# Attention steps dealt out behind whole matmul outputs instead of within them

## The chip, the cores and the metric

The kernel runs on one core of a Trainium2 chip. The metric is the device time of one execution in microseconds (us). Five engines of the core matter here: PE (TensorE, matmuls and the loads of their weights), DVE (VectorE), ACT (ScalarE), POOL (GpSimd) and SP (SyncE, which here only issues DMAs). Each engine works through its own list of instructions in order, and semaphores hold one engine until another has got far enough. Matmul results land in PSUM, which the kernel uses as eight banks of 128 x 512 floats.

## The reference

The input x has 2048 tokens of 448 numbers. It is normalised, and two branches of the normalised xn are added to it:

```python
xn = _layernorm(x, axis=-1)
return x + _A_ref(xn, A_wq, A_wk, A_wv, A_wo, A_beta) + _B_ref(xn, B_w_gate, B_w_up, B_w_down)
```

Branch B is a gated feed-forward net, `(sigmoid(xn @ w_gate) * (xn @ w_up)) @ w_down` with 1792 hidden features. Branch A is attention with 16 heads of 28 numbers over four segments of 512 tokens. In each segment a head computes `p = softmax(q k^T * scale + mask)` (the mask leaves a query only the keys at its own place or before it) and `p @ v`, mixes it with what a running memory of the earlier segments recalls (`num / den`, with a gate from beta), and the mixed heads are multiplied by `wo`.

## The kernel before

**Tiling.** Tokens come in four blocks of 512 (`xs[b]`, transposed, 128 features per piece), each of four tiles of 128 tokens. A matrix number is held as a high and a low part, and a product of two such numbers is built from several matmuls that add up in one PSUM bank: eleven for an output with 448 inputs (`TERMS`), six for the sum `down` over two groups of 128 hidden features.

**Stages.** A front part (to about 150 us) normalises x and makes queries, keys and values, and the memory's recall. Then comes the loop, to about 664 us, and then the last output projections. In the loop PE carries two streams that are interleaved by hand:

- the feed-forward net, a generator `gated()`: for each pair of hidden groups `f0`, for each token block `b`, four *outputs* of eleven products (`pgu`, L248: gate and up of each group; each is 128 x 512), and behind each output one *sum* of six products (`pd`, L173, in `down`, 128 x 448), which DVE adds to `acc` (L176). Behind an `up` output ACT takes the tanh of the gate (L256), DVE and ACT make the hidden value `hh` of it (L257, L259, L260).
- attention, a generator `attention()`: 16 *units* (a segment and four heads), each of two *pairs* of heads. A unit has 14 *steps*, listed in `SLOT`. Five steps a pair are scores steps (L612: one 512-wide matmul; or one 384 and one 128 wide; or two 256 wide, into one bank `st`). ACT copies the bank into `w` (L616, L619), POOL masks its diagonal block (L627), DVE takes maxima (L629, L633). When a pair's scores are done, five further *parts* run, one at each of the next five steps: the maxima are combined in a chain of short steps that go between DVE and POOL (L643 to L653), spread out (`mb`, L656), subtracted from `w` in three pieces (L666, DVE), and each piece goes through the exponential (L667, ACT). At step 6 of the next unit comes `finish` with `pa` (L687): 16 products per key block and head, 2.36 us of PE when nothing is late, that read the weights of both pairs.

**Order of the work.** PE and SP follow the order in which the program gives their instructions (`manual_schedule`). The orders of ACT, DVE and POOL are laid out by a scheduler from its own costs. The interleaving is decided by `yield`: the driver at L788 to L794 counts the yields of the feed-forward stream with `k`, and at every yield it runs so many attention steps that the count of steps follows `k` in proportion (234 steps over 541 counts, 0.43 a yield). Before the change an output yields three times (after its 4th, its 8th and its last product) and a sum twice (after its 3rd product and after the addition to `acc`).

**Banks.** Scores rotate through two banks (tag `s`), so a scores step needs the bank of the second scores step ahead of it, which is free once ACT has copied it. `pgu` of the gate and every second `pd` share two banks (`gu`), `pgu` of the up side has two (`p`), the other `pd` one, and `pa` one (`m`).

Of the kernel before, what the change touches and what calls it, by code (L numbers as in the profile page):

```python
# [61 lines left out]
def kernel(  # L62
# [21 lines left out]
    def split(hi, lo, src):  # L84
        A.activation(hi, src, AF.Copy)
        V.tensor_sub(lo, src, hi.bitcast(F32))

    def split_weights(w, raw):
        split(w[:, 0:4, :], w[:, 4:8, :], raw)
# [25 lines left out]
    def bank(name, tag):  # L115
        return ps.tile([P, L], F32, name=name, tag=tag, bufs=banks[tag])
# [29 lines left out]
    def eight_k(dtype, name):  # L146
        return mid.tile([P, 8, 256], dtype, name=name, tag="8k")

    def four_k(dtype, name):
        return mid.tile([P, 2, L], dtype, name=name, tag="4k", bufs=4)  # L150

    def two_k(name):
        return mid.tile([P, L], F32, name=name, tag="2k", bufs=2)
# [7 lines left out]
    def late_pair(name):  # L161
        return late.tile([P, 2, D], F32R, name=name, tag="late")
# [3 lines left out]
    def gated():  # L166

        def down(b, hs, wd, t, tag="pd"):
            tok = slice(t * P, (t + 1) * P)
            mms = [(h[:, a, tok], wd[f][:, w, :]) for f, h in hs for a, w in ((0, 0), (0, 1), (1, 0))]  # L170
            pd = bank("pd", tag)
            for n, (l, r) in enumerate(mms):
                T.matmul(pd[:, :D], l, r, start=n == 0, stop=n == len(mms) - 1)  # L173
                if n == 2:
                    yield
            V.tensor_add(acc[b][:, t, :], pd[:, :D], acc[b][:, t, :])  # L176
            yield

        raw_up, raw_down, wgu, wdn = {}, {}, {}, {}

        def load_up(f):

            raw_up[f] = mid.tile([P, 1024], F32, name="raw", bufs=2)
            if f < NF:
                nc.sync.dma_start(raw_up[f], w_ffn[f][:, :1024])
            else:
                nc.sync.dma_start(raw_up[f][:, :2 * D], w_o[:, 2 * D * (f - NF):2 * D * (f - NF + 1)])

        def load_down(f, tag="rawd"):
            raw_down[f] = (mid.tile([P, 1024], F32, name="raw", bufs=2)[:, :D] if tag == "raw" else  # L190
                           mid.tile([P, D], F32, name="rawd", bufs=1))
            nc.sync.dma_start(raw_down[f], w_ffn[f][:, 1024:])

        def ready_up(f):
            wgu[f] = eight_k(F32R, "wgu")
            split_weights(wgu[f], raw_up[f].rearrange("p (c n) -> p c n", c=4))

        def ready_down(f):
            wdn[f] = late_pair("wdn")
            split(wdn[f][:, 0, :], wdn[f][:, 1, :], raw_down[f])  # L200

        def ready_out(h):
            wo[h] = eight_k(F32R, "wo").rearrange("p c n -> p (c n)")[:, 16:]
            split(wo[h][:, :2 * D], wo[h][:, 2 * D:4 * D], raw_up[NF + h][:, :2 * D])

        begin.extend([lambda: ready_down(0), lambda: (ready_down(1), load_down(2)), lambda: ready_down(2)])
        load_up(0)
        yield
        ready_up(0)
        yield  # L210
        load_up(1)
        load_down(0)
        yield


        todo = [None, None]
        for f0 in range(0, NF, FG):


            ahead = {}  # L220
            if f0 == 0:
                ahead[0, 0] = lambda: (load_down(1, "raw"), ready_up(1))
                ahead[0, 2] = lambda: load_up(2)
                ahead[1, 3] = lambda: load_up(3)
            if f0 + FG < NF:
                ahead[1, 2] = lambda: ready_up(f0 + 2)
                if f0 > 0:
                    ahead[2, 1] = lambda: ready_down(f0 + 2)
                ahead[2, 3] = lambda: load_down(f0 + 3)
                ahead[2, 2] = lambda: load_up(f0 + 4)  # L230
                ahead[3, 2] = lambda: ready_up(f0 + 3)
                ahead[3, 3] = lambda: ready_down(f0 + 3)
                if f0 > 0:
                    ahead[0, 2] = lambda: (load_up(f0 + 3), load_down(f0 + 2))
            else:

                ahead[0, 2] = lambda: load_up(f0 + 3)
                ahead[1, 2] = lambda: ready_out(0)
                ahead[3, 2] = lambda: ready_out(1)
            for b in range(NB):  # L240
                hs = []
                for f in range(f0, f0 + FG):
                    pgu = []
                    for side in range(2):
                        slot = 2 * (f - f0) + side
                        dst = bank("pgu", ("gu", "p")[side])
                        for n, (a, w) in enumerate(TERMS):
                            T.matmul(dst, wgu[f][:, w, side * P:(side + 1) * P], xs[b][:, a, :],  # L248
                                     start=n == 0, stop=n == len(TERMS) - 1)
                            if n in (3, 7):  # L250
                                yield
                        pgu.append(dst)
                        if side == 1:

                            sg = two_k("sg")
                            A.activation(sg, pgu[0], AF.Tanh, scale=0.5)  # L256
                            V.scalar_tensor_tensor(sg, sg, 1.0, pgu[1], op0=ALU.add, op1=ALU.mult)  # L257
                            hh = four_k(F32R, "hh")
                            A.activation(hh[:, 0, :], sg, AF.Copy, scale=0.5)  # L259
                            V.scalar_tensor_tensor(hh[:, 1, :], sg, 0.5, hh[:, 0, :].bitcast(F32),  # L260
                                                   op0=ALU.mult, op1=ALU.subtract)
                            hs.append((f, hh))
                        yield
                        if todo and f0 + b > 0:
                            yield from todo.pop(0) or ()
                        if (b, slot) in ahead:
                            ahead[b, slot]()
                end = f0 + FG == NF and b == NB - 1
                todo += [down(b, hs, wdn, t, ("pd", "s" if end else "gu")[t % 2]) for t in range(NT)]
        rest.extend(todo)  # L270
# [5 lines left out]
    with tc.tile_pool(name="front", bufs=2) as sb, tc.manual_schedule(engines=FRONT):  # L276
# [200 lines left out]
        for t in range(2):  # L477
# [23 lines left out]
                        compare_op=ALU.is_ge, fill=0.0)  # L501

        ffn = gated()
        for b in range(NB):
            last = b == NB - 1
# [23 lines left out]
            for k, c in enumerate((3, 4, 5, 6, 0, 1, 2) if last else range(7)):  # L529
# [34 lines left out]
                n = k - 1 if b == 0 else k + 1  # L564
# [269 lines left out]
```

## Time and profile before

| what | value |
|---|---|
| median of 3 runs | 691.52 us (691.22 to 691.61) |
| the profiled execution's own time | 691.24 us |
| its span, first to last instruction | 689.6 us |
| PE busy over the span | 682.4 us, 99% |
| DVE busy | 569.7 us, 83% |
| ACT busy | 342.6 us, 50% |
| POOL busy | 146.0 us, 21% |

The busy time of PE is that of modelled, overlapping matmuls: what a matmul costs is read from the distance between the starts of neighbours, not from its own duration. In a timeline, consecutive instructions of one kind are merged into a row with a count; the bracket at the end is the idle time of the engine ahead of the row and what ended it. PEld is the loading of matmul weights, which runs ahead of the products.

### The profile page before, as it was taken

Reading aid. Unit: us, or ns where it says so; the run is one execution under the profiler, and the core shown is the slowest. Engines: PE = TensorE matmul, PEld = TensorE weight load, DVE = VectorE, ACT = ScalarE, POOL = GpSimd, SP = SyncE. Lnnn points to the kernel's source line nnn. Section 1 sums busy time; section 2 is a strip of 40 time slices with the busy share of each in tenths; the row PEclk is TensorE's granted clock in tenths of the full one; section 3 lists DMA queues with packets and bytes.
Section 4 is the critical chain, followed back from the end, with each engine's and each line's share of the span. In section 5 each row is a group of like instructions: output and inputs, shape, how many; then the busy total and the mean of one; then the engine's idle time right before and its main releaser. Section 6 shows DMA issues by size and latency. Waiting matters only on the chain.

```text
span 689.6 us, 10445 instructions
## 1 busy us (share of the span) xinstructions
PE 682.4 (99%) x3594; PEld 565.6 (82%) x3594; DVE 569.7 (83%) x994; ACT 342.6 (50%) x563; POOL 146.0 (21%) x349
## 2 busy tenths in 40 slices
PE   8999999999999999999999999999999999999997
PEld 7898888778878787788878878787787878878897
DVE  6765795767889898989898989998889889889863
ACT  5837555343455555544555446455544555446220
POOL 4500020101222122221222223222232322222000
PEclk9999999999999999999999999999999999999999
DMA  7446566696243233333233342324342432333342
GB/s 266 183 146 240 194 224 235 255 331 161 77 102 95 61 86 86 81 112 102 56 71 103 70 123 56 101 55 116 81 114 56 96 72 71 86 95 80 91 155 106
DMA packets 45797, 84.37 MB, mean 122 GB/s; under 512 B 6321, under 2 KB 20401, under 8 KB 45233
## 3 DMA queue, kind: packets, MB, share of 16 engines
q1 hardware_dynamic: 42736, 76.37, 35.9%
q0 software_dynamic: 3008, 7.34, 4.9%
q8 instruction: 28, 0.46, 0.3%
q14 instruction: 25, 0.20, 0.1%
HBM read 51.05 MB, written 32.64 MB: 121 GB/s over the span
## 4 chain that ended last, share of the span: by engine, by line
PE 77%; DVE 10%; issue 7%; POOL 3%; ACT 1%; DMA 1%; SPq 0%; POOLq 0%; ACTq 0%
PE pgu L248 30%; PE pd L173 14%; PE pp L355 10%; PE po L771 5%; PE pv L335 5%; PE st L612 4%; PE pa L687 4%; DVE mx L629 2%; POOL w L627 2%; PE pmm L383 2%; PE n L401 1%; DVE acc L176 1%; DVE w L666 1%; DMA acc<-in_x 1%; PE pt L95 1%
## 5 line engine op out<-in xcount | busy, mean ns | idle before, releaser
L248 PE MATMUL pgu<-xs,wgu 128*128 128x512 f32 x1232 | 316.8, 395 | 0.0
L248 PEld LDWEIGHTS pgu<-xs,wgu 128*128 128x128 f32 x1232 | 226.6, 188 | 45.0 <-issue 3.2
L173 PE MATMUL pd<-wdn,hh 128*128 128x448 f32 x672 | 161.8, 367 | 0.0
L667 ACT ACTIVATE w<-w 128x1024 f32<-128x1024 f32 (+1 forms) x96 | 87.1, 915 | 96.5 <-DVE w L666 95.8
L173 PEld LDWEIGHTS pd<-wdn,hh 128*128 128x128 f32 x672 | 123.0, 188 | 14.5 <-issue 0.6
L627 POOL TENSOR_SCALAR_AFFINE_SELECT w<-w 128x256 f32<-128x256 f32 (+1 forms) x160 | 79.1, 496 | 251.5 <-ACT w L616 216.3
L666 DVE TENSOR_TENSOR w<-w,mb 128x1024 f32<-128x1024 f32 (+1 forms) x96 | 99.7, 1050 | 0.2
L616 ACT ACTIVATE w<-st 128x512 f32<-128x512 f32 x128 | 74.8, 588 | 41.3 <-PE st L612 41.2
L629 DVE TRANSPOSE_TENSOR_REDUCE mx<-w 128x32 f32<-128x1024 f32 x64 | 79.1, 1235 | 12.9 <-POOL w L627 12.8
L355 PE MATMUL pp<-xs,wqk 128*128 128x512 f32 x308 | 77.7, 401 | 0.0
L176 DVE TENSOR_TENSOR acc<-pd,acc 128x448 f32<-128x448 f32 x112 | 67.4, 602 | 2.0 <-PE pd L173 2.0
L355 PEld LDWEIGHTS pp<-xs,wqk 128*128 128x128 f32 x308 | 56.8, 188 | 13.4 <-issue 2.4
L612 PE MATMUL st<-qk 84*128 84x128 f32 (+3 forms) x256 | 64.1, 311 | 0.4 <-ACT w L616 0.3
L259 ACT ACTIVATE hh<-sg 128x512 fp32r<-128x512 f32 x56 | 35.1, 626 | 47.3 <-DVE sg L257 37.3
L612 PEld LDWEIGHTS st<-qk 84*128 84x128 f32 x256 | 48.4, 189 | 9.3 <-ACT w L616 1.9
L256 ACT ACTIVATE sg<-pgu 128x512 f32<-128x512 f32 x56 | 33.2, 593 | 33.4 <-PE pgu L248 32.9
L656 DVE STREAM_TRANSPOSE mb<-top 128x1024 f32<-128x1024 f32 x32 | 39.8, 1243 | 10.3 <-POOL top L653 10.1
L362 DVE TENSOR_TENSOR qk<-pp,qk 128x512 fp32r<-128x512 f32 x28 | 19.3, 688 | 29.8 <-ACT e L360 23.7
L257 DVE SCALAR_TENSOR_TENSOR sg<-sg,pgu 128x512 f32<-128x512 f32 x56 | 37.4, 668 | 4.3 <-PE pgu L248 4.3
L260 DVE SCALAR_TENSOR_TENSOR hh<-sg,hh 128x512 fp32r<-128x512 f32 x56 | 38.4, 685 | 2.4 <-ACT hh L259 2.2
L335 PE MATMUL pv<-wv,xs 128*128 128x448 f32 x176 | 39.8, 376 | 0.2
L687 PE MATMUL pa<-w,vv 128*32 128x128 f32 (+3 forms) x512 | 39.6, 436 | 0.1
(100 smaller groups left out, 637.3 us busy)
## 6 DMA issues: line engine op xcount, KB each, us to landing
qk<-qd SPq DMA_DIRECT2D x192, 112.0 KB
qd<-qk SPq DMA_DIRECT2D x28, 512.0 KB
raw<-in_w_ffn SPq DMA_DIRECT2D x14, 512.0 KB
vd<-vst SPq DMA_DIRECT2D x4, 1024.0 KB
vv<-vd SPq DMA_DIRECT2D x16, 256.0 KB
od<-w POOLq DMA_DIRECT2D x16, 256.0 KB, 3.8
sums<-od SPq DMA_DIRECT2D x32, 128.0 KB
out<-acc SPq DMA_DIRECT2D x16, 224.0 KB
```

The costliest lines, as they stand in the source:

```text
L173: T.matmul(pd[:, :D], l, r, start=n == 0, stop=n == len(mms) - 1)
L176: V.tensor_add(acc[b][:, t, :], pd[:, :D], acc[b][:, t, :])
L248: T.matmul(dst, wgu[f][:, w, side * P:(side + 1) * P], xs[b][:, a, :], start=n == 0, stop=n == len(TERMS) - 1)
L335: T.matmul(pv[:, :D], xs[b][:, a, t * P:(t + 1) * P], wv[w], start=n == 0, stop=n == len(TERMS) - 1)
L355: T.matmul(pp, wqk[c][:, w, :], xs[b][:, a, :], start=n == 0, stop=n == len(TERMS) - 1)
L612: T.matmul(st[:, at:at + L - kb * P], self.qk[:KS, 1, h, kb * P:(kb + 1) * P], self.qk[:KS, 0, h, kb * P:], start=True, stop=True)
L616: A.activation(w, st, AF.Copy)
L627: G.affine_select(d, d, pattern=pattern, base=0, channel_multiplier=-1, compare_op=ALU.is_ge, fill=MASK)
L629: V.tensor_reduce(mx[:, 16 * (n - 1):16 * (n + 1)], w3[:, n // 2, :2 * L].rearrange("p (b n) -> p b n", n=32), axis=mybir.AxisListType.X, ...
L666: V.tensor_sub(w, w, m)
L667: A.activation(w, w, AF.Exp, scale=SCALE)
L687: T.matmul(pa[32 * j:32 * j + 32, kb * P:], self.vv[:, kb, 32 * j:32 * j + 32], self.pairs[j // 2].block(j % 2, kb), start=kb == 0, stop=k ...
```

## The change

In the loop the yields that stood within an output and within a sum are moved behind them. From the second token block on (`f0 + b > 0`) an output yields three times in a row behind its last product, and a sum twice in a row behind its addition. The first token block keeps its old places. The number of yields, and so `k`, stays the same: each attention step is tied to the same count, but that count now lies at the end of the output or sum. The yields in `project()`, within the last projections, stay.

```diff
@@ def down(b, hs, wd, t, tag="pd"):
             for n, (l, r) in enumerate(mms):
                 T.matmul(pd[:, :D], l, r, start=n == 0, stop=n == len(mms) - 1)
-                if n == 2:
-                    yield
             V.tensor_add(acc[b][:, t, :], pd[:, :D], acc[b][:, t, :])
+            yield
             yield
@@ gated(), the loop over outputs
                             T.matmul(dst, wgu[f][:, w, side * P:(side + 1) * P], xs[b][:, a, :],
                                      start=n == 0, stop=n == len(TERMS) - 1)
-                            if n in (3, 7):
+                            if n in (3, 7) and f0 + b == 0:
                                 yield
...
                             hs.append((f, hh))
-                        yield
+                        for _ in range(1 if f0 + b == 0 else 3):
+                            yield
                         if todo and f0 + b > 0:
                             yield from todo.pop(0) or ()
```

What it moves on PE is seen behind the first `pa`, at the second half of unit 1 (`qk_1948` is the second pair of that unit, `xs_65` a token block). Before:

```order
L248 MATMUL pgu<-xs_65,wgu 128x512 x4
L612 MATMUL st<-qk_1948 128x512
L248 MATMUL pgu<-xs_65,wgu 128x512 x7
L612 MATMUL st<-qk_1948 128x384
L612 MATMUL st<-qk_1948 128x128
L173 MATMUL pd<-wdn,hh 128x448 x6
L612 MATMUL st<-qk_1948 128x512
L248 MATMUL pgu<-xs_65,wgu 128x512 x11
```

Now:

```order
L247 MATMUL pgu<-xs_65,wgu 128x512 x11
L612 MATMUL st<-qk_1948 128x512
L612 MATMUL st<-qk_1948 128x384
L612 MATMUL st<-qk_1948 128x128
L173 MATMUL pd<-wdn,hh 128x448 x6
L612 MATMUL st<-qk_1948 128x512
L247 MATMUL pgu<-xs_65,wgu 128x512 x11
```

The output is whole, and two scores steps stand side by side behind it; the third follows six products later. On PE again, ahead of `pa` of unit 1 (`qk_2076` before and `qk_2080` now are the same pair of unit 2). Before:

```order
L612 MATMUL st<-qk_2076 128x384
L612 MATMUL st<-qk_2076 128x128
L173 MATMUL pd<-wdn,hh 128x448 x3
L248 MATMUL pgu<-xs_66,wgu 128x512 x4
L612 MATMUL st<-qk_2076 128x256 x2
L248 MATMUL pgu<-xs_66,wgu 128x512 x7
L687 MATMUL pa<-w,vv 32x512 x4
```

Now:

```order
L612 MATMUL st<-qk_2080 128x384
L612 MATMUL st<-qk_2080 128x128
L247 MATMUL pgu<-xs_66,wgu 128x512 x11
L612 MATMUL st<-qk_2080 128x256 x2
L687 MATMUL pa<-w,vv 32x512 x4
```

`pa` follows the scores step directly; the seven products that stood between them now stand ahead of both. The last place is DVE between the last scores of unit 1 and the weights that its `pa` reads: from the combination of the maxima (L645) to the third subtraction (L666, `128x2x2x128`). Before:

```order
L645 TENSOR_TENSOR mx<-mx 128x2x8
L649 TENSOR_TENSOR mx<-mx,up 64x2x16
L176 TENSOR_TENSOR acc_72<-pd,acc_72 128x448
L651 TENSOR_TENSOR top<-mx,up 32x32
L656 STREAM_TRANSPOSE mb<-top 128x1024
L666 TENSOR_TENSOR w<-w,mb 128x2x512
L629 TENSOR_REDUCE mx<-w 128x32
L257 SCALAR_TENSOR_TENSOR sg<-sg,pgu 128x512
L176 TENSOR_TENSOR acc_72<-pd,acc_72 128x448
L666 TENSOR_TENSOR w<-w,mb 128x2x2x256
L260 SCALAR_TENSOR_TENSOR hh<-sg,hh 128x512
L666 TENSOR_TENSOR w<-w,mb 128x2x2x128
```

Now, where the first `acc` addition stands ahead of L645:

```order
L645 TENSOR_TENSOR mx<-mx 128x2x8
L649 TENSOR_TENSOR mx<-mx,up 64x2x16
L651 TENSOR_TENSOR top<-mx,up 32x32
L656 STREAM_TRANSPOSE mb<-top 128x1024
L256 SCALAR_TENSOR_TENSOR sg<-sg,pgu 128x512
L666 TENSOR_TENSOR w<-w,mb 128x2x512
L259 SCALAR_TENSOR_TENSOR hh<-sg,hh 128x512
L629 TENSOR_REDUCE mx<-w 128x32
L174 TENSOR_TENSOR acc_72<-pd,acc_72 128x448
L666 TENSOR_TENSOR w<-w,mb 128x2x2x256
L174 TENSOR_TENSOR acc_72<-pd,acc_72 128x448
L666 TENSOR_TENSOR w<-w,mb 128x2x2x128
```

One addition to `acc` more stands ahead of the third subtraction, between it and the second, and L649 and L651, which each wait for a short step of POOL, have nothing between them any more.

## The prediction

> **What bounds the kernel.** I read the page first (its busy times are in the table above), then the busy time of the loop (160 to 660 us), then what PE waited for there, then PE's timeline.
>
> ```profile
> 160.00:660.00 500.00, 499.48 (x2667) 409.73 (x2667) 445.39 (x724) 254.36 (x400) 121.99 (x306) 1.00 0.34 87
> ```
>
> The columns behind the window are its length and the busy time of PE, PEld, DVE, ACT and POOL, then the granted clock. PE is busy for 499.5 of 500 us at a clock of 1.00, DVE for 89%. That PE looks busy doesn't show that its products flow at their pace, so the waits of its weight loads in the loop come next (total, times, longest):
>
> ```profile
> PEld st L612 <- ACT w L616: 1.9, 4, 0.7
> PEld pa L687 <- POOL w L627: 1.7, 5, 0.4
> PEld pa L687 <- ACT w L667: 1.4, 2, 0.8
> ```
>
> What stops PE is small: four scores steps that waited for a bank (ACT's copy, L616), and `pa`, which waited for the last weights (ACT's exponential, L667). So PE bounds the loop, and the change is worth what it does to the pace of PE's products and to these two waits. Products, loads and bytes stay the same, and the names in SP's and POOL's DMA queues come in the same order as before, so no load is moved past another.
>
> **Part 1: whole outputs.** PE's timeline (start, length, instruction) with outputs and sums that scores steps break, and with whole ones:
>
> ```profile
> 306.62 1.08 PE L248 MATMUL pgu<-xs,wgu 128*128 128x512 f32 x4
> 307.54 0.40 PE L612 MATMUL st<-qk 84*128 84x512 f32 x1
> 307.77 1.79 PE L248 MATMUL pgu<-xs,wgu 128*128 128x512 f32 x7
> 309.40 0.77 PE L173 MATMUL pd<-wdn,hh 128*128 128x448 f32 x3
> 310.01 0.40 PE L612 MATMUL st<-qk 84*128 84x384 f32 x2
> 310.25 0.82 PE L173 MATMUL pd<-wdn,hh 128*128 128x448 f32 x3
> 310.90 1.08 PE L248 MATMUL pgu<-xs,wgu 128*128 128x512 f32 x4
> ...
> 628.00 0.40 PE L612 MATMUL st<-qk 84*128 84x384 f32 x2
> 628.23 1.42 PE L173 MATMUL pd<-wdn,hh 128*128 128x448 f32 x6
> 629.49 0.40 PE L612 MATMUL st<-qk 84*128 84x256 f32 x2
> ...
> 632.26 1.37 PE L173 MATMUL pd<-wdn,hh 128*128 128x448 f32 x6
> 633.47 2.68 PE L248 MATMUL pgu<-xs,wgu 128*128 128x512 f32 x11
> 635.99 1.37 PE L173 MATMUL pd<-wdn,hh 128*128 128x448 f32 x6
> ```
>
> By starts, a whole output takes 635.99 - 633.47 = 2.52 us. The broken one takes 0.92 + 1.63 = 2.55 without the 0.23 us of its scores step: the break costs 0.03. The broken sum takes 0.61 + 0.65 = 1.26, and a whole sum behind such a pair of scores products (384 and 128 wide) takes 629.49 - 628.23 = 1.26 too, against 1.21 behind an output: the 0.05 belong to whatever follows the pair, and this break is free. The order before has 68 broken outputs and 37 broken sums that are whole afterwards, 105 breaks at 0 to 0.03 us, so 0 to 3.2 us. Free breaks are the pairs and most of the sums, and the full price falls on outputs that a 512-wide scores step breaks, about a third of all; I take 0.011 each, **-1.1 us**.
>
> **Part 2: scores steps side by side.** No two scores steps are adjacent before; afterwards 14 couples are. A step needs the bank of the second one ahead. Counting PE's products between them, the closest such distance before is 3.3 us; afterwards it is 1.7 us at five places (one whole sum between the couple and the third step) and 3.0 at five more. Against this stands the time from the start of a scores step to the end of its copy:
>
> ```profile
> 307.97 0.60 ACT L616 ACTIVATE w<-st 128x512 f32<-128x512 f32 x1 [0.43 <-PE st L612]
> ```
>
> ```profile
> 296.03 0.40 PE L612 MATMUL st<-qk 84*128 84x512 f32 x1
> 299.43 0.58 ACT L616 ACTIVATE w<-st 128x512 f32<-128x512 f32 x1
> 300.06 0.50 PE L612 MATMUL st<-qk 84*128 84x512 f32 x1 [0.28 <-ACT w L616]
> 598.72 0.40 PE L612 MATMUL st<-qk 84*128 84x384 f32 x2
> 600.50 0.58 ACT L616 ACTIVATE w<-st 128x512 f32<-128x512 f32 x1
> 620.20 0.40 PE L612 MATMUL st<-qk 84*128 84x512 f32 x1
> 623.29 0.58 ACT L616 ACTIVATE w<-st 128x512 f32<-128x512 f32 x1
> ```
>
> When ACT is free the copy ends 308.57 - 307.54 = 1.03 us after the step's start. In the second fence, the first step has its copy done after 3.98 us, and the step that needs its bank stands idle at 300.06. The four bank waits before exceed their distances by 0.95 us in all. The long times are those of steps in mid-unit, where exponentials that wait for DVE stand ahead of the copy in ACT's list; steps 0, 8 and 9 of the ten mostly have 1.0 to 1.8. Where do the ten tight places fall? Mostly on those quick steps. Taking for each step the time that the same step has before, only three of the ten are late: one by 0.08, the one at 598.72 by 2.36 - 1.68 = 0.68, and the one at 620.20 by 3.67 - 2.99 = 0.68; two old places stay late by 0.4. That is 1.85 against 0.95: **+0.9 us**. The bounds are -0.95 (all bank waits vanish) and, with 2.5 us (the middle of 1.03 and 3.98) at each of the five closest places, 5 x 0.8 more.
>
> The Trainium skill ("Perfetto Trace Analysis", section "Matmuls") says that independent groups of matmuls should rotate through different PSUM banks, so that the evacuation of one overlaps the next one's products. By that rule two rotating banks cover the couples and this term would be nothing or a gain; the wait at 300.06 shows that here two banks cover no copy that comes 3.98 us late.
>
> **Part 3: `pa` and its weights.** All 16 `pa` take 2.36 us but these:
>
> ```profile
> 289.17 3.10 PE L687 MATMUL pa<-w,vv 128*32 128x512 f32 x32
> 319.25 2.45 PE L687 MATMUL pa<-w,vv 128*32 128x512 f32 x32
> 436.85 3.28 PE L687 MATMUL pa<-w,vv 128*32 128x512 f32 x32
> 467.06 2.36 PE L687 MATMUL pa<-w,vv 128*32 128x512 f32 x32
> 584.94 2.50 PE L687 MATMUL pa<-w,vv 128*32 128x512 f32 x32
> ```
>
> Lost before: 0.74 + 0.09 + 0.92 + 0.14 = 1.89 us. Why, at the first:
>
> ```profile
> 290.11 0.62 ACT L667 ACTIVATE w<-w 128x512 f32<-128x512 f32 x1
> 290.78 1.22 PEld L687 LDWEIGHTS pa<-w,vv 128*32 128x32 f32 x20 [0.61 <-ACT w L667]
> ```
>
> The third exponential ends at 290.73, and only then go the loads for the second key block, which would have gone 0.61 earlier, 1.0 us after the start of `pa`. Units 1 and 9, which don't wait, have their last exponential end at 229.88 and 466.12, against 230.48 and 467.06 for the starts of their `pa`:
>
> ```profile
> 228.10 1.78 ACT L667 ACTIVATE w<-w 128x1024 f32<-128x1024 f32 x2 [0.60 <-DVE w L666]
> 230.48 2.36 PE L687 MATMUL pa<-w,vv 128*32 128x512 f32 x32
> 465.50 0.62 ACT L667 ACTIVATE w<-w 128x512 f32<-128x512 f32 x1
> ```
>
> So their room is 1.6 and 1.9 us. Now the change: counted in PE's products, `pa` of nine units comes 0.6 to 0.9 us sooner after the last scores that it needs, that of five units 0.6 to 1.6 later. And DVE's list between those scores and the last subtraction changes: the pieces of unit 1 shown with the change have one addition more, and two steps of the chain between DVE and POOL lie bare. The prices:
>
> ```profile
> L176 DVE TENSOR_TENSOR acc<-pd,acc 128x448 f32<-128x448 f32 x112 | 67.4, 602 | 2.0 <-PE pd L173 2.0
> ```
>
> ```profile
> DVE mx L649 <- POOL up L648: 10.3, 26, 0.7
> DVE top L651 <- POOL up L650: 7.0, 23, 0.5
> ```
>
> An addition is 0.60 us, a bare step (10.3 + 7.0) / 49 = 0.35. Unit 1 loses 0.7 (sooner) + 0.6 + 0.3 = 1.6, all its room. Unit 9 loses about 1.1 and keeps 0.8. The same count for all sixteen leaves five units late by 1.74 in all, where the same measure gives four and 1.65 before: **+0.1 us**. Bounds: -1.9 (no unit waits), and, if each of the nine sooner ones loses what the first and third long rows lose (0.83), 7.5 - 1.9 = +5.6.
>
> **Sum:** 691.24 - 1.1 + 0.9 + 0.1 = 691.1 us against the profiled execution. The median of the runs shown is 0.28 higher, so I forecast **691.4 us** on its scale. A difference under 0.2% (1.4 us) is about what a measurement of this kernel can't tell from none; that is 690.1 to 692.9.
>
> **Rivals.**
> *Slower by `pa`.* The weights must be earlier in nine units, and DVE, with 89% busy and 17 us of waits at two steps of its chain, has little to give. If half of the nine wait 0.83 each, that is 3.7 instead of 2.0: 693.1 us. From four waiting units on it decides. Against it: units with a large room (1.6, 1.9) among the nine, and that a stop of PE gives DVE time to catch up.
> *Slower by banks.* Two copies now reach ACT together and the second waits 0.58 us for the first. With 0.8 us at each of the five closest places and the old 0.95 besides, the bank waits are 5.0 instead of 1.85: 694.5 us. For it speaks the row at 299.43; against it, that the tight places fall on steps with quick copies.
> *Faster.* DVE's lists leave 54 of the 96 chain steps bare instead of 66, which is 12 x 0.35 = 4 us less idle time there. If that brings subtractions forward, both waits of PE shrink: with all of them gone, 691.52 - 1.1 - 0.95 - 1.89 = 687.6; with half, 689.0 us. Against it: the count of unit 1, whose chain becomes longer.
>
> **Chances.** Forecast (within 0.2%) 0.38; slower by `pa` 0.22, slower by banks 0.15; faster 0.25. So faster 0.25, same 0.38, slower 0.37. The range runs from 688.5 (most of the waits gone) to 694.8 (the bank rival with a little of the other); the forecast's own is 690.1 to 692.9.
>
> **What would show it.** Part 1: whole outputs at 2.52 by starts, no gain elsewhere in them. Part 2: waits of scores steps for ACT's copies of about 2 us in PE, at the couples with one sum behind them. Part 3: `pa` rows above 2.36 us at units that had none, unit 1 among them, about 2 us in all. Wrong would be: more than six `pa` rows over 2.4 us, bank waits over 4 us, a new wait of `pgu` or `pd` for its bank, or a broken output that was dearer than 0.03 us.

## The result, and the profile after

The changed kernel takes 689.50 us (median of 6 runs, 689.35 to 689.86) against 691.50 us before. The ratio is 0.9971, with a 95% interval of 0.9961 to 0.9982: 2.0 us or 0.29% faster. The runs of each kernel lie within 0.7 us, so less than the 1.4 us that the prediction allowed can be told from none. The forecast of 691.4 us ("within 0.2%", 690.1 to 692.9) missed that by 1.9 us; the wide range of 688.5 to 694.8 holds it, and the rival called *Faster* comes nearest in time, though, as will be seen, not by its mechanism.

The same views of the changed kernel. The loop, 160 to 660 us (length; PE, PEld, DVE, ACT, POOL busy; clock):

```profile
160.00:660.00 500.00, 499.79 (x2678) 411.52 (x2676) 445.50 (x728) 254.32 (x400) 127.36 (x306) 1.00 0.34 88
```

What PE's weight loads waited for in the loop (total, times, longest):

```profile
...
PEld pa L687 <- ACT w L667: 2.1, 4, 0.8
...
PEld pa L687 <- POOL w L627: 0.7, 2, 0.4
...
PEld st L612 <- ACT w L616: 0.3, 1, 0.3
```

Busy times say nothing: both kernels show PE at 100% and DVE at 89%. The waits do: those of scores steps for a bank have nearly gone (1.9 us in four before, 0.3 in one now), those of `pa` for its weights are much as they were. PE's timeline with whole groups:

```profile
301.84 2.65 PE L247 MATMUL pgu<-xs,wgu 128*128 128x512 f32 x11
304.33 0.40 PE L612 MATMUL st<-qk 84*128 84x384 f32 x2
304.56 1.42 PE L173 MATMUL pd<-wdn,hh 128*128 128x448 f32 x6
305.82 0.40 PE L612 MATMUL st<-qk 84*128 84x256 f32 x2
306.06 2.69 PE L247 MATMUL pgu<-xs,wgu 128*128 128x512 f32 x11
308.59 0.40 PE L612 MATMUL st<-qk 84*128 84x512 f32 x1
308.82 1.38 PE L173 MATMUL pd<-wdn,hh 128*128 128x448 f32 x6
310.04 0.40 PE L612 MATMUL st<-qk 84*128 84x384 f32 x2
```

By starts a whole output takes 304.33 - 301.84 = 2.49 and 308.59 - 306.06 = 2.53 us, a sum 1.26 behind a pair of scores products (304.56 to 305.82) and 1.22 behind a 512-wide one (308.82 to 310.04). And `pa`, 2.36 us where nothing is late:

```profile
230.56 2.36 PE L687 MATMUL pa<-w,vv 128*32 128x512 f32 x32
289.05 3.33 PE L687 MATMUL pa<-w,vv 128*32 128x512 f32 x32
435.95 3.26 PE L687 MATMUL pa<-w,vv 128*32 128x512 f32 x32
495.62 2.60 PE L687 MATMUL pa<-w,vv 128*32 128x512 f32 x32
```

**An account of PE's time.** PE stops for other work at these two waits alone, so its time from the first output of the second token block to its last product can be added up from the distances between the starts of neighbouring matmuls. A product's bare distance is 227 ns (output), 199 (sum), or 228, 172, 58 and 116 (scores products of 512, 384, 128 and 256 columns). What goes beyond it is put down to *pace* (small excesses of outputs, sums and scores products), *bank* (a scores step that starts late) or *`pa`* (what a `pa` takes beyond its undisturbed 2.29 us to the next start). The rest, such as what follows a 128-wide product, is alike in all kernels within 0.2 us, but for the one run whose clock fell (below). In us:

| kernel | PE's region | pace | bank | `pa` | bank + `pa` |
|---|---|---|---|---|---|
| before | 527.61 | 6.40 | 0.87 | 1.90 | 2.77 |
| after | 525.67 | 4.99 | 0.08 | 2.11 | 2.19 |

The region is 1.94 us shorter: 1.41 by pace, 0.79 by the bank waits, -0.21 by `pa`, the rest -0.05. The pace splits into 0.66 at outputs, 0.38 at sums and 0.37 at the scores products themselves.

Most of that last share is not one of whole groups. A scores product that had to wait for its bank takes about 0.11 us more to the next start than one that came in time, in every kernel here. At unit 4 before:

```profile
300.06 0.50 PE L612 MATMUL st<-qk 84*128 84x512 f32 x1 [0.28 <-ACT w L616]
300.40 0.86 PE L248 MATMUL pgu<-xs,wgu 128*128 128x512 f32 x3
```

From start to start that is 0.34 us, against 0.23 above (308.59 to 308.82). The kernel before has four such products, 0.44 us of excess, the changed one has one, 0.11. Counted with the waits that they follow, the change gains 1.09 us by pace and 1.11 at the banks. The tables leave these products in the pace; without them it is 5.97 before and 4.88 after.

### The profile page after: what moved, and what is told of

Same layout as the page of the kernel before. It is cut to its first block, busy times and chain, and to the rows that moved or that the text cites. A ratio compares the mean times of both kernels' runs of the same rounds, so it can differ in the third digit from the quotient of the medians.

```text
span 687.7 us, 10438 instructions
## 1 busy us (share of the span) xinstructions
PE 681.7 (99%) x3594; PEld 566.6 (82%) x3594; DVE 567.4 (83%) x994; ACT 342.6 (50%) x563; POOL 151.3 (22%) x349
## 4 chain that ended last, share of the span: by engine, by line
PE 70%; DVE 14%; issue 9%; POOL 4%; DMA 1%; ACT 1%; SPq 0%; POOLq 0%; ACTq 0%
PE pgu L247 26%; PE pd L173 13%; PE pp L355 10%; PE po L771 5%; PE pv L335 5%; PE st L612 3%; PE pa L687 3%; DVE mx L629 3%; DVE w L666 2%; POOL w L627 2%; DVE acc L174 2%; PE pmm L383 2%; PE n L401 2%; DVE hh L259 1%; DVE mx L633 1%
## 5 line engine op out<-in xcount | busy, mean ns | idle before, releaser
L247 PE MATMUL pgu<-xs,wgu 128*128 128x512 f32 x1232 | 304.1, 394 | 0.0
L173 PE MATMUL pd<-wdn,hh 128*128 128x448 f32 x672 | 156.0, 367 | 0.0
L627 POOL TENSOR_SCALAR_AFFINE_SELECT w<-w 128x256 f32<-128x256 f32 (+1 forms) x160 | 81.2, 509 | 236.4 <-ACT w L616 183.6
L666 DVE TENSOR_TENSOR w<-w,mb 128x1024 f32<-128x1024 f32 (+1 forms) x96 | 98.9, 1045 | 0.1
L629 DVE TRANSPOSE_TENSOR_REDUCE mx<-w 128x32 f32<-128x1024 f32 x64 | 79.0, 1235 | 17.0 <-POOL w L627 17.0
L612 PE MATMUL st<-qk 84*128 84x128 f32 (+3 forms) x256 | 61.9, 312 | 0.0
```

The source lines that it names most:

```text
L612: T.matmul(st[:, at:at + L - kb * P], self.qk[:KS, 1, h, kb * P:(kb + 1) * P], self.qk[:KS, 0, h, kb * P:], start=True, stop=True)
L627: G.affine_select(d, d, pattern=pattern, base=0, channel_multiplier=-1, compare_op=ALU.is_ge, fill=MASK)
L629: V.tensor_reduce(mx[:, 16 * (n - 1):16 * (n + 1)], w3[:, n // 2, :2 * L].rearrange("p (b n) -> p b n", n=32), axis=mybir.AxisListType.X, ...
L666: V.tensor_sub(w, w, m)
```

## Experiments: one half of the change at a time, and another division

Theory A: whole groups bring pace, and the arrangement that came out happens to have few waits. Rival B: breaks cost nothing, the waits alone moved. Rival C: DVE's chain sets the time, and PE stops for it at one place or another.

**Outputs whole, sums broken.** The changed kernel with `down` as before:

```diff
                 T.matmul(pd[:, :D], l, r, start=n == 0, stop=n == len(mms) - 1)
+                if n == 2:
+                    yield
             V.tensor_add(acc[b][:, t, :], pd[:, :D], acc[b][:, t, :])
-            yield
             yield
```

> Only the outputs of eleven products are made whole; the sums of six are still broken after their third product. Theory A (whole groups let PE's products flow at a better pace, and the arrangement happens to have fewer bank waits): the 68 unbroken outputs give about 0.67 us and the scores steps' own share about 0.2, so about 690.6 us if the waits of before stay, with the excess of the output products in PE's timeline down from 3.1 to about 2.5 us in the loop. Rival B (breaks cost nothing, only the waits for banks and for the weights moved): the output products keep their excess of 3.1 us, and the time differs from before only by what the bank and weight waits differ.

Measured: 690.83 us, ratio 0.9988 (0.9979 to 0.9996).

**Sums whole, outputs broken.** The kernel before, with the opposite edit in `down` alone.

> Only the sums of six products are made whole; the outputs are broken as before. Theory A: 37 unbroken sums give about 0.4 us, plus some 0.15 of the scores steps between, so about 691.0 us if the waits stay. Rival B: no change of the pace of the sum products (1.9 us excess in the loop), a time that follows the waits alone.

Measured: 691.81 us, ratio 1.0003 (0.9994 to 1.0012).

**Two and three.** The changed kernel with two yields behind an output and three behind a sum:

```diff
-                        for _ in range(1 if f0 + b == 0 else 3):
+                        for _ in range(1 if f0 + b == 0 else 2):
...
             V.tensor_add(acc[b][:, t, :], pd[:, :D], acc[b][:, t, :])
             yield
             yield
+            yield
```

> All groups whole as in the changed kernel, but the five counts of an output and its sum are divided two and three instead of three and two, so the same whole groups carry the attention steps at other places (14 couples of scores steps, five of them with one sum behind, as in the changed kernel). Theory A: the pace is that of the changed kernel, 1.4 us better than before; the waits can differ by about 1 us, so 689 to 691 us. Rival B: the gain was the one arrangement's luck; the pace gains nothing and the time lies at 691 or above.

Measured: 691.50 us, ratio 0.9998 (0.9989 to 1.0007): with every group whole, nothing gained. The account of the three:

| kernel | PE's region | pace | bank | `pa` | bank + `pa` |
|---|---|---|---|---|---|
| outputs whole | 526.93 | 4.80 | 0.08 | 3.54 | 3.62 |
| sums whole | 528.05 | 6.22 | 0.85 | 2.59 | 3.44 |
| two and three | 527.59 | 5.25 | 2.04 | 1.71 | 3.75 |

Rival B falls: where the outputs are whole the pace is 4.8 to 5.3, where they are broken 6.2 to 6.4, and without the products behind a bank wait 4.69 to 4.91 and 5.97 to 6.00. The 68 unbroken outputs alone bring 1.60 us, or 1.28 without these products, 19 ns each with the scores steps and sums around them. The 37 unbroken sums bring 0.18, where 0.55 was expected, and that is two such products fewer (0.22): the sums bring nothing of their own. But the time follows the waits as much. *Two and three*, expected at 689 to 691 us, has the pace, and its waits, 1.0 us above those of the kernel before, take the gain away. With outputs whole, `pa` of unit 3 stops PE so long that its row breaks in two:

```profile
289.08 1.70 PE L688 MATMUL pa<-w,vv 128*32 128x512 f32 x12
291.91 0.52 PE L688 MATMUL pa<-w,vv 128*32 128x384 f32 x4 [1.13 <-ACT w L668]
```

## Experiments: taking the waits away

**`pa` a step later.** The changed kernel with

```diff
-SLOT = (0, 0, 0, None, 0, 0, 2, 3, 1, 1, 1, None, 1, 1)
+SLOT = (0, 0, 0, None, 0, 0, None, 2, 3, 1, 1, 1, 1, 1)
```

> The changed kernel with the product of the weights and the values (finish) one attention step later, and the pause between the scores steps of a unit's second pair taken out for it. Theory A: the three long products (0.97 + 0.90 + 0.24 = 2.1 us lost) come down to 2.36 us each, and the time falls to about 687.4 us unless the denser scores steps bring bank waits. Rival C (the time is set by DVE's chain, and PE waits for it at one place or another): the waits come back at scores steps or at the product, and the time stays within 0.5 us of 689.5.

Measured: 690.47 us, ratio 0.9984 (0.9975 to 0.9993). Not 687.4, and slower than the changed kernel. The waits of its weight loads:

```profile
...
PEld st L612 <- ACT w L616: 3.7, 8, 1.6
...
PEld pa L687 <- POOL w L627: 1.4, 4, 0.4
...
PEld pa L687 <- ACT w L667: 0.3, 1, 0.3
```

The `pa` waits did go (0.41 us left of 2.11). But with the pause gone, the five scores steps of a unit's second pair follow one another, and six scores steps, four of them in second pairs, now wait for banks (2.58 us instead of 0.08). The pace is 5.30. Both forecasts missed the time, and since the edit made these steps denser, the run doesn't tell theory A from rival C.

**The same, with the pause filled by the second half of `finish`.**

```diff
-SLOT = (0, 0, 0, None, 0, 0, 2, 3, 1, 1, 1, None, 1, 1)
+SLOT = (0, 0, 0, None, 0, 0, None, 2, 1, 1, 3, 1, 1, 1)
```

> The changed kernel with the first half of finish (the weights-times-values product) one step later, as in the earlier run, but the second half put where the pause in the second pair was, so that the scores steps there are less dense. Theory A (waits are a matter of the places, each can be removed by itself): the long products come down to 2.36 us (2.1 us gained) with under 0.5 us of bank waits, so about 687.8 us. Theory C (DVE's chain sets it): bank waits of 2 us come back as in the earlier run, about 690 us.

Measured: 695.84 us, ratio 1.0053 (1.0039 to 1.0067): far off, for a reason that the edit brought along. PE and ACT at one of two such places, and the clock in stretches behind it:

```profile
398.05 0.40 PE L612 MATMUL st<-qk 84*128 84x384 f32 x2
400.39 0.50 PE L612 MATMUL st<-qk 84*128 84x512 f32 x1 [1.94 <-ACT w L616]
400.73 2.09 PE L173 MATMUL pd<-wdn,hh 128*128 128x448 f32 x6
402.61 3.59 PE L247 MATMUL pgu<-xs,wgu 128*128 128x512 f32 x11
```

```profile
399.74 0.60 ACT L616 ACTIVATE w<-st 128x512 f32<-128x512 f32 x1 [0.80 <-DMA od<-w]
```

```profile
400.00:402.00 2.00, 1.61 (x6) 1.45 (x7) 0.64 (x4) 1.80 (x4) 0.92 (x5) 0.78 0.85 209
402.00:404.00 2.00, 2.00 (x7) 1.63 (x6) 1.74 (x2) 0.00 (x0) 0.85 (x3) 0.50 0.02 8
406.00:410.00 4.00, 4.00 (x21) 3.50 (x21) 4.00 (x6) 2.98 (x5) 0.66 (x1) 1.00 0.20 56
```

The copy of the next unit's first scores goes into the `w` out of which the second half of `finish` sends its result, and that DMA now leaves too late: the copy waits for `od<-w`. So this run says nothing on theories A and C. In the profiled execution, which took 697.19 us, bank waits are 5.81 us, and 2.88 more are products at a lower clock (see the end).

**A third bank where the bank waits were.** The kernel before, with the second scores step of each unit's second pair put into the bank of `pa`:

```diff
-                st = bank("st", "s")
+                st = bank("st", "m" if n == 1 and self.odd else "s")
```

(`self.odd` is the pair's number modulo 2.)

> The kernel before, but of each unit the second scores step of its second pair uses the bank of the weights-times-values product, which is idle then, so the step behind it finds its bank free. All four bank waits of before (0.87 us in PE) fell on such a step that waited for a copy standing behind an exponential. If those waits were a true cost, they go and the time falls by 0.9 us to about 690.7. If PE only moves its stop to another place (DVE's chain sets the time), the weights-times-values products get longer by as much and the time stays at 691.5.

Measured: 691.70 us, ratio 1.0000 (0.9992 to 1.0009). PE at unit 4, where before a scores step stood until 300.06:

```profile
299.77 0.40 PE L613 MATMUL st<-qk 84*128 84x512 f32 x1
...
318.82 3.25 PE L688 MATMUL pa<-w,vv 128*32 128x512 f32 x32
```

The step no longer waits, and `pa` of the same unit, 2.45 us before, takes 3.25. Over the kernel the bank waits fall from 0.87 to 0.34 and `pa` rises from 1.90 to 2.99, at a pace of 6.07. PE came to `pa` 0.4 us sooner and the weights did not: the last exponential ends at 320.53, before at 320.16, although ACT, DVE and POOL have the same lists in both kernels. That is rival C at this place: removing the stop ahead only moved it. Why the weights came no sooner is not shown.

## Experiments: the same kernels, shifted

If the waits depend on where the steps fall, a mere shift must change them. `LEAD` and `TAIL` set the count at which attention starts and ends; moving both by one or two keeps the rate:

```diff
-LEAD, TAIL = 15, 53
+LEAD, TAIL = 16, 52
```

Both kernels were run one count later, the changed one also one and two counts earlier (14, 54 and 13, 55) and two later (17, 51).

> The kernel before with all attention steps given one count later (a shift of the start, the rate unchanged): the broken outputs stay broken, the steps fall on other places. Theory A: the pace excess stays at about 6.4 us, the waits for banks and weights come out at another sum, 1 to 5 us instead of 2.8: 690 to 694 us.

> The changed kernel with the same shift by one count. Theory A: the pace excess stays at about 5.0 us, so 1.4 us better than the shifted kernel before, and the waits come out at another sum, 1 to 5 us instead of 2.2: 689 to 692 us. If instead whole outputs as such brought the whole gain of 2.0 us, this kernel is 2.0 us faster than the shifted one before.

> The changed kernel with all attention steps one count earlier. Pace excess about 5.0 us, waits between 1 and 4 us: 688.4 to 691.4 us.

> The changed kernel with all attention steps given two counts earlier. Whole groups keep the pace excess at about 5.0 us; the waits come out between 1 and 4 us. With waits of 1 us it would be the fastest so far, 688.4 us; with the mean of the runs so far (3 us) 690.4.

> The changed kernel with all attention steps two counts later. Pace excess about 5.0 us, waits between 1 and 4 us: 688.4 to 691.4 us. Together with the other shifts this gives the scatter of the waits for whole groups.

| kernel | median, us | ratio to before (95%) | pace | bank | `pa` | bank + `pa` |
|---|---|---|---|---|---|---|
| before, one later | 689.79 | 0.9972 (0.9961 to 0.9982) | 6.28 | 1.21 | 0.05 | 1.26 |
| after, one later | 690.21 | 0.9979 (0.9970 to 0.9988) | 5.02 | 1.57 | 1.34 | 2.91 |
| after, one earlier | 690.75 | 0.9991 (0.9983 to 1.0000) | 5.35 | 2.16 | 1.00 | 3.16 |
| after, two earlier | 690.53 | 0.9988 (0.9979 to 0.9996) | 4.90 | 0.47 | 2.88 | 3.35 |
| after, two later | 690.16 | 0.9982 (0.9973 to 0.9991) | 5.27 | 1.48 | 1.08 | 2.56 |

This is the main finding. The kernel *before*, with its outputs broken, is 1.8 us faster when its steps come one count later, just below what was expected: its `pa` hardly waits. That is nearly the whole gain of the change, without the change. Shifted alike, the two kernels stand at 689.79 and 690.21, and the change is 0.4 us *slower*: it still gains 1.26 of pace but takes 1.65 more of waits. Over five places the changed kernel's waits are 2.2 to 3.4 us, and the place that was measured as its result is the lowest of them: in this the 2.0 us owe something to luck. The pace is steadier. Without the products behind a bank wait it is 4.64 to 4.91 us in the eight kernels with whole outputs so far whose clock held, and 5.96 to 6.00 in the four with broken ones.

**All counts behind the output.** The changed kernel with five yields behind an output and none behind a sum in the loop, for the rival that couples of scores steps stall at their banks:

> All groups whole, and all five counts stand behind the output, none behind the sum: 61 couples of scores steps instead of 14, and five places with three side by side, where the third needs the bank of the first at once. Theory A: the pace is as good as in the changed kernel (excess about 5.0 us) or a little better, and the waits grow: each of the five triples stops PE for at least the 0.6 us that a copy takes beyond its distance, 3 us or more in all, so about 692 us or slower. Rival (couples as such do no harm): within 1 us of 689.5.

Measured: 694.65 us, ratio 1.0054 (1.0041 to 1.0067).

```profile
PE st L613 <- ACT w L617: 4.9, 4, 2.0
PE st L613 <- ACT w L620: 0.5, 1, 0.5
```

The pace becomes the best of all (3.35 us; why it is so low isn't shown, though the work changes its kind least often here), and bank waits of 6.84 us more than eat it up. Here two banks hold a couple, not three in a row.

## Why the prediction was right or wrong, point by point

**What bounds the kernel: right.** The differences come from the pace of PE's products and from the two waits alone. The region less pace, bank and `pa` comes to 518.4 to 518.6 us in every run but the one whose clock fell.

**Part 1, pace: right.** Forecast -1.1 us, measured -1.41, of which 0.32 are products behind a bank wait and belong to part 2; without them -1.09. Broken outputs were the costly kind and broken sums free, as read from the rows: 19 ns and nothing where I took 11 for both. That the sum came out so well is partly luck: only 24 of the 105 breaks are outputs broken by a 512-wide step, a quarter and not a third, which at 0.03 would give 0.7.

**Part 2, scores steps side by side: wrong, and this is the step that failed.** Forecast +0.9, measured -0.79, or -1.11 with the products behind the waits. The profiled execution came in 1.7 us below the sum (689.46 against 691.1), and this term alone was off by as much. The distances were right, and the ten tight places did fall on quick copies; the one wait left is 0.08 us. What failed is "taking for each step the time that the same step has before". Four waits before lay behind step 5 (the first of the second pair) of units 4, 13, 14 and 15. ACT's list, which can be read without a run, shows why: in these units the first exponential of the unit's first pair stands ahead of that copy, in units 4, 5, 8, 9, 13, 14 and 15 in all. At unit 4 before, this row stands between the step at 296.03 and its copy at 299.43:

```profile
298.47 1.06 ACT L667 ACTIVATE w<-w 128x1024 f32<-128x1024 f32 x1 [6.76 <-DVE w L666]
```

In the changed kernel that exponential stands ahead in units 8, 10, 12 and 14; there the copy ends 2.7 to 3.8 us after its step, and the step that needs the bank comes 4.27 us after it, in time. At unit 4 afterwards:

```profile
296.12 0.40 PE L612 MATMUL st<-qk 84*128 84x512 f32 x1
296.55 0.60 ACT L616 ACTIVATE w<-st 128x512 f32<-128x512 f32 x1 [4.75 <-PE st L612]
299.55 1.06 ACT L667 ACTIVATE w<-w 128x1024 f32<-128x1024 f32 x1
300.39 0.40 PE L612 MATMUL st<-qk 84*128 84x512 f32 x1
```

The copy goes at once and the exponential 3.0 us later; before, the copy ended 3.98 us after its step. At unit 15 it ends 1.04 us after its step instead of 3.67, at the step 8 of unit 14 that I had priced at 0.68, 1.35 instead of 2.36. The Trainium skill ("PSUM — Partial Sum Buffer", section "Engine vs sequencer instructions") says that ScalarE's queue is a strict FIFO; the rows agree, since before at unit 4 a copy whose scores are ready stands behind an exponential that has waited for DVE. Here the moved steps changed the scheduler's lists, and a latency that is made of queueing has to be read from the new list, not carried over.

**Part 3, `pa`: right in size, with luck in the places.** Forecast +0.1, measured +0.21. The count for unit 1 (all its room of 1.6 us lost) came out: its last exponential ended 0.60 us ahead of `pa` before and 0.80 us behind its start now, a loss of 1.4, and PE just did not stop, so the long row that I had named for unit 1 did not come. Of the units that stop, 3 and 8 stayed and 10 came for 4 and 13: three late, where I had five.

**The rivals.** *Slower by `pa`* and *slower by banks* were wrong for this arrangement, but both happen in others: `pa` loses 3.54 us with only the outputs whole, the banks 2.04 with two and three and 6.84 with five and none. *Faster* was near in time (689.0) by luck, for its mechanism did not occur: DVE's waits in the chain fell by 3 us, near the 4 that were counted, but came back at its reductions. The weights were not earlier: from a unit's last scores step to the end of its last exponential it is 13.8 us on average, before 13.7. Before:

```profile
DVE mx L629 <- POOL w L627: 12.8, 26, 1.3
...
DVE mb L656 <- POOL top L653: 10.1, 18, 0.7
```

After:

```profile
DVE mx L629 <- POOL w L627: 17.0, 27, 2.2
...
DVE mb L656 <- POOL top L653: 10.1, 19, 0.7
DVE mx L649 <- POOL up L648: 8.0, 21, 0.7
DVE top L651 <- POOL up L650: 6.2, 19, 0.6
```

With the two rows shown in the prediction (10.3 and 7.0), the three steps of the chain waited 27.4 us before against 24.3 here, and the reduction L629 12.8 against 17.0.

**What stays open.** Why one arrangement waits 1.3 us in all and another 3.8 is explained place by place, not predicted: it hangs on the lists of three engines at once. Whether whole groups are better *on average* over arrangements isn't settled; the pace says 1.1 to 1.2 us better, the one shifted pair says 0.4 us worse in all, and the kernel before was run at two places only. Why a product behind a bank wait takes 0.11 us longer is open too.

## What to carry to other kernels

In a kernel whose bounding engine is full, split the time into the pace of that engine's work and its waits, by the distances between starts; here the first was a property of the edit, the second of the arrangement. Before an edit of the order is credited with a gain of some tenths of a per cent, shift both kernels by a step or two: here a shift alone was worth 1.8 us, and turned the comparison around. A latency that contains queueing does not stay with its instruction when the lists change.

## What the runs showed of the hardware

Two stops of PE of about 2 us were followed by a lower clock for some microseconds. In the profiled execution of the run with the pause filled, a stop of 1.94 us was followed by a granted clock of 0.78 and then 0.50 over the next 4 us, and the output behind it took 3.59 us in its row instead of 2.65; the second stop (2.19 us, to 550.93 us) did the same. In the profiled execution with all counts behind the output, two stops of about the same length (1.8 to 2 us) left the clock at 1.00. It varies from one execution to the next: the five of the first kernel had mean clocks of 0.995 to 1.000 and took 694.69 to 697.19 us, the longest at the lowest clock; of the five of the second, two had 0.998 and took 695.9 and 696.29 us, the others 1.000 and at most 694.65. The Trainium skill ("TensorE: Matmul & The Clock Gate", section "What's actually happening") has the clock fall back after at least one idle window of about 3.4 us; here it fell after less. No such dip occurs in the profiled executions before and after, whose clock is 1.00 over the loop.
